# Three raw weight buffers, loads one piece further ahead, sums of w1 and w2 in common slabs, and first parts of w_out on ACT

## The chip, the core and the metric

The kernel runs on one core of one Trainium2 chip. The metric is device time in microseconds (us): the median over runs of the time from start to end of the program. Five engines share a core's on-chip memory: PE multiplies matrices, DVE and ACT work on tiles elementwise, POOL helps with copies, and SP issues the transfers from and to device memory.

## The reference: attention and two feed-forward layers

```python
# attention: q, k, v are (4, 8, 768, 64) float32; 4 sinks, a window of 128
scores = (1 / np.sqrt(64)) * np.matmul(q, k.transpose(0, 1, 3, 2))
keep = is_sink | in_window                      # column < 4, or 0 <= row - column < 128
scores = np.where(keep, scores, -1000000000.0)
a = np.exp(scores - np.max(scores, axis=-1, keepdims=True))
a = a / (np.sum(a, axis=-1, keepdims=True) + 1e-09)
x = np.matmul(a, v)                             # laid out as 3072 tokens x 512
h = np.maximum(x @ w_in, 0.0)                   # w_in 512 x 2048
x = (h * h @ w_out).astype(np.float32)          # w_out 2048 x 512
return ((x @ w1) * (x @ w2) @ w3) @ w_out2      # w1, w2 512 x 1024; w3 1024 x 1024; w_out2 1024 x 512
```

All weights arrive as float64, the rest as float32.

## The kernel before

**Stages.** The 3072 tokens are cut into 6 blocks of 512 (n = 0 to 5), and each block into 16 steps (j = 0 to 15), one per 128 columns of `w_in`. A step multiplies the block by its columns of `w_in` (`ffn_A`, 12 products into `hps`), applies the squared relu (`ffn_act1` to `ffn_act3`, which make `r` and `g`), and multiplies the step before by 128 rows of `w_out` (`ffn_B`, 12 products into `x1ps`). Between these stands one unit of attention, for the next block: score products into `sc`, masking and row maxima on DVE (`pr`), exponentials on ACT, a transpose by transfer (`pt<-ph`), the product with v into `y`, the division on DVE (`xn`), and a transposition on PE (`y<-ident,xn`). The unit runs as a pipeline over several steps, and the products with v and the transposition share the bank `y`. So a step's `y<-vp,pt` on PE can't start before DVE has read the bank's former content in `xn`; behind `y` on PE stands the next step's `hps`.

The prelude (0 to 94.6 us) computes the first 16 units in another way, directly in float32, and converts 12 weight pieces. Block n = 0 (94.6 to 212 us, called stage 0 here) converts the rest of `w_in` and `w_out`, 20 pieces, while it computes. Blocks 1 to 4 (212 to 610 us) convert two pieces of `w1` and `w2` each, in steps 4 and 5. Block 5 has no attention; it converts `w_out2` and the rest of `w1`, `w2`, and after it `w3` and `w_out2` are folded into one matrix (610 to 748 us). The rest (748 to 1108 us) is the second layer, in a form with seven block products in place of eight, for which sums of blocks of `w1` and `w2` are wanted.

**A weight piece.** A piece is 512 KB of float64. `f32_piece` (L1012) takes a buffer of the ring `raw64`, which has two, and has SP load it (L1029). `f64_to_f32_up` (L83) turns it into float32 in four instructions: ACT makes the magnitude (L86, `cvy<-raw`), DVE two integer pieces (L91 and L94, `cvt<-raw`) and merges them (L97, `cvy<-cvy,cvt`). The raw buffer is free once L86, L91 and L94 have read it. `split` (L795) then makes two half-precision parts: the first is a rounded copy of the float32 piece, by ACT or, where `hi_eng` is DVE, by DVE (CAST `wo<-cvy`); the second is the difference, on DVE or POOL (`wo<-cvy,wo`). `conv_wo` gives the first part of `w_out` to DVE in j = 0 to 7 and to ACT in j = 8 to 15.

**Ahead.** `w_load(upto)` issues loads up to a count, `w_conv` converts the next loaded piece. In the prelude and in blocks 0 to 4 the load of piece i + 2 is issued after the conversion of piece i. Block 5 does the same with a list of items (`item_load`).

**Sums.** `conv_w12` (L1221) waits for both pieces of a pair, then writes four sums of blocks (`s1` to `s4`) into one slab `w12s` of 128 x 1024, and splits that slab with one ACT and one DVE instruction. The ring `t2` has eight buffers of 128 x 512 float32, taken by `cvy`, `cvt`, the relu output `r` and others.

**What sets the order.** A scheduler orders the program by its own estimates. ACT, DVE and PE are written through a wrapper that keeps program order in blocks 0 to 4 (`InOrder`, L270), but the four instructions of `f64_to_f32_up` are not: they, SP and POOL are placed by the scheduler.

Of the kernel before, what the change touches and what calls it, by code (L numbers as in the profile page):

```python
# [7 lines left out]
F32 = mybir.dt.float32  # L8
F16 = mybir.dt.float16
BF16 = mybir.dt.bfloat16  # L10
I32 = mybir.dt.int32
# [285 lines left out]
def kernel(  # L297
# [18 lines left out]
    ACT, DVE, PE = (InOrder(tc, e, pinned) for e in (nc.scalar, nc.vector, nc.tensor))  # L316
# [4 lines left out]
    KD, KF, K2 = DM // 128, DFF // 128, DF2 // 128  # L321
# [18 lines left out]
    T2B, GB = 8, 3  # L340
# [25 lines left out]
    with ExitStack() as fast:  # L366
# [6 lines left out]
        def slab(tag, shape, dt, name, bufs=1):  # L373
            return big.tile(shape, dt, tag=tag, name=name, bufs=bufs)
# [420 lines left out]
        def split(src, hi, lo, lo_eng=None, hi_eng=None):  # L795

            if hi_eng is DVE:
                DVE.tensor_copy(out=hi, in_=src)
            else:
                ACT.activation(out=hi, in_=src, func=ACTF.Copy)  # L800
            (lo_eng or DVE).tensor_tensor(out=lo, in0=src, in1=hi, op=ALU.subtract)
# [9 lines left out]
        def ok(u):  # L811
            return 0 <= u < NU
# [204 lines left out]
        def f32_piece(src, dst=None, name="cv"):  # L1017

            if src.dtype == F32:
                if dst is None:  # L1020
                    dst = slab("t2", [128, 512], F32, name, bufs=T2B)
                SP.dma_start(out=dst, in_=src)
                return dst
            raw = slab("raw64", [128, 512, 2], I32, "raw64", bufs=2)
            fl = raw.rearrange("p n c -> p (n c)")
            sb32 = src.bitcast(I32)
            if len(sb32.shape) == 3:
                fl = fl.rearrange("p (a c) -> p a c", a=sb32.shape[1])
            SP.dma_start(out=fl, in_=sb32)  # L1029
            return raw  # L1030

        def conv(raw, dst=None):
            if raw.dtype == F32:
                ACT.activation(out=raw, in_=raw, func=ACTF.Copy, scale=W_UP)
                return raw
            y = slab("t2", [128, 512], I32, "cvy", bufs=T2B)
            if dst is None:
                dst = y.bitcast(F32)
            t = slab("t2", [128, 512], I32, "cvt", bufs=T2B)
            i = cvn[0]  # L1040
            cvn[0] += 1
            f64_to_f32_up(nc, raw, y, dst.bitcast(I32), st_w[:, i:i + 1], t)
            return dst
# [20 lines left out]
        def conv_wo(j):  # L1064
            c = j // 4
            if c not in wo_t:
                wo_t[c] = slab(f"wo{c}", [128, 2, 4, DM], F16, "wo")
            x = conv(raw_w.pop(("wo", j)))
            w = wo_t[c]
            split(x, w[:, 0, j % 4, :], w[:, 1, j % 4, :], hi_eng=DVE if j < KF // 2 else ACT)  # L1070

        hps_t = {}

# [150 lines left out]
        def conv_w12(i):  # L1224


            w12_x.append(conv(raw_w.pop(("w12", i))).rearrange("p (c f) -> p c f", c=KD))
            f, m = divmod(i, 2)
            if not m:
                return  # L1230
            x1, x2 = w12_x
            w12_x.clear()
            if f < 4:
                t = slab(f"w12_{f}", [128, 2, 7, 2, 128], F16, "w12")
                hi, lo = t[:, 0], t[:, 1]
            else:
                hi, lo = (slab(f"wi{2 * f - 8 + c}", [128, 7, 2, 128], F16, f"w12{c}") for c in range(2))
            w12_t[f] = hi, lo
            t = slab("w12s", [128, 4, 2, 128], F32, "w12s")
            s1, s2, s3, s4 = (t[:, c] for c in range(4))  # L1240
            a11, a12, a21, a22 = x1[:, 0:2], x1[:, 2:4], x2[:, 0:2], x2[:, 2:4]
            for o, p, q, op in (
                (s1, a21, a22, ALU.add), (s2, s1, a11, ALU.subtract), (s3, a11, a21, ALU.subtract),
                (s4, a12, s2, ALU.subtract),
            ):
                DVE.tensor_tensor(out=o, in0=p, in1=q, op=op)
            split(x1, hi[:, 0:2].rearrange("p a c f -> p (a c) f"), lo[:, 0:2].rearrange("p a c f -> p (a c) f"))
            split(a22, hi[:, 2], lo[:, 2])
            split(t, hi[:, 3:7], lo[:, 3:7])

        def x1_ops(o, top, bot):

# [125 lines left out]
        nl, ncv = [0], [0]  # L1378

        def w_load(upto):  # L1380
            while nl[0] < min(upto, len(pieces)):
                ld, _, j = pieces[nl[0]]
                ld(j)
                nl[0] += 1
# [36 lines left out]
        for h in range(2):  # L1421
# [1 line left out]
                out=vsf[h * NSINK:(h + 1) * NSINK, :, h, :],  # L1423
                in_=v[0].rearrange("(a h2) s d -> h2 s a d", h2=2)[h, 0:NSINK],
            )
        w_load(2)
        att_load_first(0, (0, 1, 2))
        if TBF > 2:
            att_load_first(1, (0, 1, 2))
# [3 lines left out]
        for u in range(UB + LEAD):  # L1433
            if 0 <= u - 3 < UB:
                att_norm(u - 3)
                att_X(u - 3)
                att_xT(u - 3)
            att_early(u)
            if u % 2 == 0 and u + 2 < UB:
                dir_T(u // 2 + 1)  # L1440
            if u < UB:
                dir_S(u)
                att_soft(u)
                att_exp(u)
            elif ok(u):
                att_S(u)
                att_soft(u)
                att_exp(u)
            if 0 <= u - 1 < UB:
                dir_P(u - 1)  # L1450
            if 0 <= u - 2 < UB:
                dir_O(u - 2)
            if ok(u - 2) and u - 2 >= UB:
                att_O(u - 2)
            if ok(u - 3) and u - 3 >= UB:
                att_X(u - 3)
            if ok(u) and u >= UB:
                att_P(u)
            for _ in range(2):
                if ncv[0] < L0 + 1:  # L1460
                    w_conv()
                    w_load(ncv[0] + 2)
            if u % TBF == 1 and u < UB:
                split_k(u // TBF)
            if u > TBF and (u - 1) % TBF == 0 and (u - 1) // TBF <= HP:
                split_v(u - 2)
# [4 lines left out]
        items = [(load_wo2, conv_wo2, i) for i in range(K2)]  # L1471
# [4 lines left out]
        def item_load(i):  # L1476
            items[i][0](items[i][2])
# [3 lines left out]
        for s in range(NK * KF):  # L1481
            n, j = divmod(s, KF)
            last = n == NK - 1
            e0, e1 = U0[n + 1] + LEAD, (U0[n + 2] if not last else U0[n + 1]) + LEAD
            us = list(range(uo, e0 + (e1 - e0) * (j + 1) // KF))
            uo = e0 + (e1 - e0) * (j + 1) // KF
            assert len(us) == (0 if last else 1)
            pinned[0] = not last
            if last and j == 0:
                low_att = att_verdict()  # L1490
                att_stack.close()
                late_p.append(fast.enter_context(tc.tile_pool(name="late", bufs=1)))
            ffn_A(n, j)
            for u in us:
                att_early(u)

            if n == 0:
                want = min(2 * KF, want0[j] + 1)
            elif not last:
                want = 2 * KF + 2 * (n - 1) + (j >= 4) + (j >= 5)  # L1500
            if last:
                if j == 0:
                    item_load(0)
                    item_load(1)
                items[j][1](items[j][2])
                item_load(j + 2)
            while not last and ncv[0] < want and ncv[0] < len(pieces):
                w_load(ncv[0] + 1)
                w_conv()
                w_load(ncv[0] + 2)  # L1510
            ffn_act1(n, j)
            for u in us:
                if ok(u):
                    att_S(u)
                    att_soft(u)
            ffn_sq(n, j)
            ffn_act2(n, j)
            for u in us:
                if ok(u):
                    att_exp(u)  # L1520
            ffn_act3(n, j)
            for u in us:
                if ok(u):
                    att_P(u)
            if pend:
                b = pend.pop()
                ffn_B(*b)
                if b[1] == KF - 1:
                    x1_spill(b[0])
            pend.append((n, j))  # L1530
            for u in us:
                if ok(u - 2):
                    att_O(u - 2)
                if ok(u - 3):
                    att_X(u - 3)
            if last:
                if j == KF // 2:
                    load_w3(0)
                w = wi_t[j][:, 0] if j < KF // 2 else wo_t[(j - KF // 2) // 2][:, 0, j % 2 * 2:j % 2 * 2 + 2]
                upper(w.rearrange("p c f -> p (c f)"))  # L1540
# [15 lines left out]
        for o, n in enumerate(order):  # L1556
            todo = []
            for f in range(K2):
                c = ffn_C(n, f)
# [14 lines left out]
                if f == 1 and o + 1 < NB:  # L1574
                    x = x1s_t[o + 1]
# [42 lines left out]
```

## Times and profile of the kernel before

| | us |
|---|---|
| median of 3 runs | 1110.32 (1108.42 to 1110.94) |
| the profiled execution | 1110.19 |
| its span, first to last instruction | 1108.0 |
| PE busy in the span | 1045.3 (94%) |
| DVE busy | 750.3 (68%) |
| ACT busy | 709.4 (64%) |
| POOL busy | 45.0 (4%) |

The profiled execution's time is its span and 2.2 us around it. The mean granted TensorE clock was 0.973 of full speed. Times in the rows below are us from the span's start, durations of groups are given as busy time and mean ns of one, and what stands in brackets behind an instruction is the idle time of its engine just before it, with what ended that.

### The profile page before, as it was taken

To read this page: it belongs to the slowest core of one execution; us is meant where nothing else is said; L and a number is where in the kernel's file an instruction comes from. 1 tells how busy PE (TensorE), PEld (TensorE's weight loads), DVE (VectorE), ACT (ScalarE), POOL (GpSimd) and SP (SyncE) were. 2 spreads that over 40 slices of the span, in tenths; PEclk is the share of its full clock that TensorE was granted. 3 is DMA by queue.
4 is the path that set the end of the run, shared out by engine and by line. 5 is a ranking of instruction groups with operands and counts; after the bars stand their busy time and mean duration, and the time that the engine had idled before them with its cause. 6 is when DMAs were issued, how large, how long until landed. Compare 5 with 4: busy or idle time off the path is not lost. (4 is left out here: it accounts for less than half of the span.)

```text
span 1108.0 us, 20449 instructions
## 1 busy us (share of the span) xinstructions
PE 1045.3 (94%) x7146; PEld 636.4 (57%) x7146; DVE 750.3 (68%) x2292; ACT 709.4 (64%) x1836; POOL 45.0 (4%) x163
## 2 busy tenths in 40 slices
PE   6777897999999999999999998999999999999996
PEld 5665443555555555555554444457767776777774
DVE  8797888887788888877865667945363636453433
ACT  6975688887667666766754877854464546454532
POOL 2110111000000000000000000000000000000000
PEclk9867999999999999999999999999999999999998
DMA  8876787786567657556833324421020201010101
GB/s 189 157 157 140 179 204 184 150 183 122 104 144 145 117 107 173 118 114 144 147 68 99 115 96 140 164 75 40 2 77 1 77 1 39 1 39 1 38 1 41
DMA packets 265535, 113.46 MB, mean 102 GB/s; under 512 B 237648, under 2 KB 254032, under 8 KB 264784
## 3 DMA queue, kind: packets, MB, share of 16 engines
q1 hardware_dynamic: 265136, 111.55, 43.7%
q8 instruction: 58, 0.95, 0.4%
q14 instruction: 53, 0.43, 0.2%
q10 hardware_dynamic: 288, 0.52, 0.1%
HBM read 62.08 MB, written 11.53 MB: 66 GB/s over the span
## 5 line engine op out<-in xcount | busy, mean ns | idle before, releaser
L288 PE MATMUL hps<-xT,wi 128*128 128x512 f16 x1152 | 270.9, 386 | 0.0
L288 PE MATMUL x1ps<-g,wo 128*128 128x512 f16 x1152 | 265.6, 380 | 3.0 <-ACT g L288 2.0
L288 PE MATMUL cps<-x1T,w 128*128 128x256 f16 x2016 | 231.5, 273 | 7.2 <-DVE cq L288 4.6
L288 PEld LDWEIGHTS <-w 128*128 128x128 f16 x2016 | 196.9, 98 | 44.5 <-issue 9.1
L288 PEld LDWEIGHTS <-wi 128*128 128x128 f16 x1152 | 115.0, 100 | 123.2 <-issue 8.6
L288 PEld LDWEIGHTS <-wo 128*128 128x128 f16 x1152 | 109.8, 98 | 122.6 <-issue 5.7
L288 PE MATMUL ops<-w,h 128*128 128x512 f16 x576 | 133.5, 379 | 1.8 <-ACT h L288 1.8
L288 ACT ACTIVATE cp<-cps 128x256 f32<-128x256 f32 x96 | 36.1, 376 | 131.3 <-PE cps L288 131.3
L288 ACT ACTIVATE r<-hps 128x512 f32<-128x512 f32 x96 | 56.8, 592 | 94.7 <-PE hps L288 94.7
L288 ACT ACTIVATE pr<-pr,stt 128x264 f32<-128x264 f32 (+1 forms) x176 | 77.6, 483 | 32.9 <-DVE stt L288 31.5
L288 PEld LDWEIGHTS <-h 128*128 128x128 f16 x576 | 56.2, 98 | 58.1 <-ACT h L288 2.1
L288 DVE TENSOR_TENSOR ph<-pr,ph 128x512 f16<-128x512 f32 (+2 forms) x148 | 59.2, 436 | 35.2 <-ACT ph L288 33.2
L288 DVE SCALAR_TENSOR_TENSOR asb<-cq,cps 128x256 f32<-128x256 f32 x48 | 20.2, 420 | 87.6 <-PE cps L288 87.6
L288 DVE CUSTOM_DVE_ANT_0 pr<-sc,mask 128x264 f32<-128x264 f32 (+1 forms) x176 | 65.2, 400 | 16.1 <-PE sc L288 15.5
L288 PEld LDWEIGHTS <-pt 128*128 128x128 f16 x956 | 40.3, 98 | 34.5 <-issue 17.1
L288 ACT ACTIVATE ph<-pr 128x512 f16<-128x512 f32 (+2 forms) x148 | 55.9, 421 | 5.8 <-DMA pt<-ph 3.4
L288 ACT ACTIVATE g<-r 128x512 f16<-128x512 f32 x88 | 55.3, 629 | 2.4
L288 DVE TENSOR_TENSOR g<-r,g 128x512 f16<-128x512 f32 x56 | 38.6, 689 | 24.6 <-ACT g L288 24.4
L97 DVE SCALAR_TENSOR_TENSOR cvy<-cvy,cvt 128x512 int32<-128x512 int32 x72 | 49.1, 688 | 8.5 <-ACT cvy L86 8.3
L288 PE MATMUL y<-vp,pt 128*128 128x65 f16 (+1 forms) x888 | 40.6, 195 | 14.7 <-DVE xn L288 14.6
L288 DVE TENSOR_TENSOR h<-asb,h 128x512 f16<-128x512 f32 x48 | 33.2, 691 | 28.2 <-ACT h L288 28.2
L288 PEld LDWEIGHTS <-qT 128*128 128x128 f16 x592 | 41.4, 99 | 18.9 <-issue 0.7
(193 smaller groups left out, 1490.3 us busy)
## 6 DMA issues: line engine op xcount, KB each, us to landing
raw<-in_moe_w_out_dram SPq DMA_DIRECT2D x24, 512.0 KB
raw<-in_moe_w_dram SPq DMA_DIRECT2D x24, 512.0 KB
raw<-in_moe_w_in_dram SPq DMA_DIRECT2D x16, 512.0 KB
raw<-in_k_dram SPq DMA_DIRECT2D x84, 64.0 KB
raw<-in_q_dram SPq DMA_DIRECT2D x84, 64.0 KB
raw<-in_v_dram SPq DMA_DIRECT2D x84, 64.0 KB
x_dr<-x1e SPq DMA_DIRECT2D x20, 256.0 KB
x1s<-x_dr SPq DMA_DIRECT2D x5, 1024.0 KB
```

The source lines that it names most:

```text
L97: nc.vector.scalar_tensor_tensor(out=dst, in0=y, scalar=3, in1=t, op0=ALU.logical_shift_left, op1=ALU.bitwise_or)
L288: r = f(*args, **kw)
```

## The change

The ring of raw buffers has three in place of two, and all loads are issued one piece further ahead: three at the start, and piece i + 3 after the conversion of piece i. ACT makes the first part of all 16 `w_out` pieces. The four sums of a pair go into two slabs of the ring `t2`, 128 x 512 each, in place of one slab of their own, and are split by two ACT and two DVE instructions of half the width. In block 5 three items are loaded at the start.

```diff
-            raw = slab("raw64", [128, 512, 2], I32, "raw64", bufs=2)
+            raw = slab("raw64", [128, 512, 2], I32, "raw64", bufs=3)
...
-            split(x, w[:, 0, j % 4, :], w[:, 1, j % 4, :], hi_eng=DVE if j < KF // 2 else ACT)
+            split(x, w[:, 0, j % 4, :], w[:, 1, j % 4, :], hi_eng=ACT)
...
-            t = slab("w12s", [128, 4, 2, 128], F32, "w12s")
-            s1, s2, s3, s4 = (t[:, c] for c in range(4))
+            t = [slab("t2", [128, 2, 2, 128], F32, "w12s", bufs=T2B) for _ in range(2)]
+            s1, s2, s3, s4 = (t[c // 2][:, c % 2] for c in range(4))
...
-            split(t, hi[:, 3:7], lo[:, 3:7])
+            for c in range(2):
+                split(t[c], hi[:, 3 + 2 * c:5 + 2 * c], lo[:, 3 + 2 * c:5 + 2 * c])
...
-        w_load(2)
+        w_load(3)
         att_load_first(0, (0, 1, 2))
...
                     w_conv()
-                    w_load(ncv[0] + 2)
+                    w_load(ncv[0] + 3)
...
                     item_load(1)
+                    item_load(2)
                 items[j][1](items[j][2])
-                item_load(j + 2)
+                if j + 3 < len(items):
+                    item_load(j + 3)
             while not last and ncv[0] < want and ncv[0] < len(pieces):
                 w_load(ncv[0] + 1)
                 w_conv()
-                w_load(ncv[0] + 2)
+                w_load(ncv[0] + 3)
```

The change moves instructions. At the start of the prelude, in SP's queue, this is the difference (L518 are the attention's first large loads):

```order
 L1029 DMA raw_183<-in_moe_w_in_dram 128x4x256
 L1029 DMA raw_185<-in_moe_w_in_dram 128x4x256
-L518 DMA raw_187<-in_k_dram 128x6x64 x2
-L518 DMA raw_190<-in_q_dram 128x6x64 x2
+L1029 DMA raw_187<-in_moe_w_in_dram 128x4x256
+L518 DMA raw_189<-in_k_dram 128x6x64 x2
+L518 DMA raw_192<-in_q_dram 128x6x64 x2
```

A third weight piece stands ahead of the attention's first large loads.

In SP's queue at the head of stage 0 the kernel before has this (qT, pt and `raw<-in_k` belong to the attention):

```order
L594 DMA_TRANSPOSE qT<-pkq 128x4x128
L1029 DMA raw_1408<-in_moe_w_out_dram 128x1024
L1029 DMA raw_1515<-in_moe_w_out_dram 128x1024
L738 DMA_TRANSPOSE pt<-ph_101 128x9x128
L1029 DMA raw_1525<-in_moe_w_in_dram 128x4x256
L506 DMA raw<-in_k_dram 128x2x64 x2
```

At the same place the changed kernel has this:

```order
L1029 DMA raw_1410<-in_moe_w_out_dram 128x1024
L1029 DMA raw_1517<-in_moe_w_in_dram 128x4x256
L1029 DMA raw_1527<-in_moe_w_out_dram 128x1024
L738 DMA_TRANSPOSE pt<-ph_101 128x9x128
L506 DMA raw<-in_k_dram 128x2x64 x2
```

The three loads that stood here begin with the piece that stood second, so each place in the queue carries the next piece.

On DVE, in one step of the middle of stage 0, the kernel before has this between the transposed tile `xT` and the packing of keys `pkk` (`den` is the row sum, `xn` the division):

```order
L288 TENSOR_TENSOR xT_1281<-y,xT_1280 128x128
L288 TENSOR_SCALAR den_1903<-y 128x2
L288 RECIPROCAL den_1903<-den_1903 128x2
L288 TENSOR_TENSOR xn<-y,den_1903 128x128
L288 SCALAR_TENSOR_TENSOR pkk<-raw,pkk 128x4x64 x2
```

In the same step the changed kernel has this (`ISA pr` is the masking with the row maximum):

```order
L288 TENSOR_TENSOR xT_1283<-y,xT_1282 128x128
L288 TENSOR_SCALAR den_1905<-y 128x2
L91 TENSOR_SCALAR cvt<-raw_1826 128x512
L288 ISA pr,stt<-sc,mask 128x128
L288 ISA stt 128x1
L94 TENSOR_SCALAR cvt<-raw_1826 128x512
L288 ISA pr,stt<-sc,mask 128x128
L288 ISA stt 128x1
L288 RECIPROCAL den_1905<-den_1905 128x2
L97 SCALAR_TENSOR_TENSOR cvy<-cvy,cvt 128x512
L288 TENSOR_SCALAR stt<-stt 128x2
L288 TENSOR_TENSOR xn<-y,den_1905 128x128
```

A conversion and the masking of the next unit have moved ahead of the division `xn` in this step. The two kernels have the same order on PE from stage 0 to the last block.

## Rows read from the trace of the kernel before

**Rows 1.** Windows by stage: start:end, length; then engines' busy time and columns named.
```profile
core 0: us, PE busy (x) PEld busy (x) DVE busy (x) ACT busy (x) POOL busy (x), PEclk, DMA share, GB/s
0.00:94.60 94.60, 69.40 (x420) 59.26 (x421) 77.25 (x358) 70.64 (x253) 14.90 (x50) 0.81 0.79 166
94.60:212.00 117.40, 103.07 (x686) 52.51 (x685) 98.21 (x318) 91.58 (x267) 11.36 (x31) 0.94 0.79 176
138.50:166.20 27.70, 25.52 (x178) 13.23 (x177) 24.34 (x76) 22.25 (x68) 3.30 (x7) 1.00 0.90 204
212.00:610.00 398.00, 398.00 (x2842) 210.73 (x2840) 310.03 (x1063) 272.76 (x687) 18.72 (x84) 1.00 0.62 128
610.00:748.00 138.00, 130.65 (x633) 63.16 (x632) 98.36 (x195) 103.08 (x218) 0.00 (x0) 0.99 0.35 118
0.00:27.70 27.70, 18.55 (x108) 15.27 (x109) 22.61 (x129) 18.51 (x65) 6.74 (x31) 1.00 0.81 189
```

**Rows 2.** Waits in stage 0 (94.6 to 212): total us, times, longest.
```profile
PE y L288 <- DVE xn L288: 13.4, 5, 3.6
...
DVE cvt L91 <- DMA raw<-in_moe_w_out_dram: 9.8, 5, 2.9
...
ACT cvy L86 <- DMA raw<-in_moe_w_out_dram: 8.2, 5, 2.8
...
ACT wo L288 <- DVE cvy L97: 2.9, 3, 2.2
```

**Rows 3.** Timeline of PE, 132 to 450: start, us, instruction, [idle before].
```profile
132.17 0.34 PE L288 MATMUL y<-vp,pt 128*128 128x65 f16 x6 [2.79 <-DVE xn L288]
...
132.50 4.44 PE L288 MATMUL hps<-xT,wi 128*128 128x512 f16 x12
...
192.84 0.34 PE L288 MATMUL y<-vp,pt 128*128 128x65 f16 x6 [2.29 <-DVE xn L288]
...
211.88 2.75 PE L288 MATMUL hps<-xT,wi 128*128 128x512 f16 x12
...
413.32 1.03 PE L288 MATMUL hps<-xT,wi 128*128 128x512 f16 x4
...
449.67 1.03 PE L288 MATMUL hps<-xT,wi 128*128 128x512 f16 x4
```

**Rows 4.** Timeline of DVE around the last gap of rows 3.
```profile
184.59 0.47 DVE L91 TENSOR_SCALAR cvt<-raw 128x512 uint16<-128x512 uint16 x1 [2.94 <-DMA raw<-in_moe_w_out_dram]
...
191.85 0.67 DVE L97 SCALAR_TENSOR_TENSOR cvy<-cvy,cvt 128x512 int32<-128x512 int32 x1
192.51 0.28 DVE L288 TENSOR_TENSOR xn<-y,den 128x128 f32<-128x128 f32 x1
```

**Rows 5.** Timeline of SP's queue: weight loads issued before that wait.
```profile
170.25 0.54 SPq L1029 DMA_DIRECT2D raw<-in_moe_w_in_dram  x1
...
180.44 0.52 SPq L1029 DMA_DIRECT2D raw<-in_moe_w_out_dram  x1
```

**Rows 6.** First part of w_out by engine, stage 0: busy, mean ns, idle before.
```profile
L288 DVE CAST wo<-cvy 128x512 f16<-128x512 f32 x6 | 2.5, 420 | 0.0
```

**Rows 7.** The same on ACT, stage 0.
```profile
L288 ACT ACTIVATE wo<-cvy 128x512 f16<-128x512 f32 x8 | 5.0, 624 | 2.9 <-DVE cvy L97 2.9
```

**Rows 8.** Splits of sums, and of a 512-wide piece, DVE, whole span.
```profile
L288 DVE TENSOR_TENSOR w<-w12s,w 128x1024 f16<-128x1024 f32 x8 | 9.8, 1220 | 1.8 <-ACT w L288 1.7
...
L288 DVE TENSOR_TENSOR w<-cvy,w 128x512 f16<-128x512 f32 x8 | 5.5, 688 | 4.8 <-ACT w L288 4.4 <-PE hps L288 0.4
```

**Rows 9.** Split of sums on ACT, whole span.
```profile
L288 ACT ACTIVATE w<-w12s 128x1024 f16<-128x1024 f32 x8 | 8.4, 1054 | 7.8 <-DVE w12s L288 7.6
```

**Rows 10.** Waits in the prelude (0 to 94.6).
```profile
DVE cvt L91 <- DMA raw<-in_moe_w_in_dram: 4.7, 3, 2.1
```

**Rows 11.** Timeline of PE in the prelude.
```profile
44.70 0.37 PE L288 MATMUL y<-ident,two 128*16 128x128 f32 x1 [1.89 <-DVE den L288]
...
54.96 0.33 PE L288 MATMUL y<-ident,xn 128*128 128x128 f32 x1 [1.64 <-DVE xn L288]
```

## The prediction

> **What bounds the kernel now.** I read the windows by stage first. From 212 to 610 us PE is busy in all of its 398.00 us, so there an edit on ACT or DVE changes nothing unless it makes PE wait [rows 1]. Stage 0 (94.6 to 212) is another matter: PE is busy in 103.07 of 117.40 us, and the DMA share is 0.79 there [rows 1]. How long it would take undisturbed can be read from later steps: the first product of a step starts at 413.32 and, six steps on, at 449.67, which is 36.35 / 6 = 6.06 us a step and 96.9 for 16 steps [rows 3]. Stage 0 is thus 117.4 - 96.9 = 20.5 us longer than its products need.
>
> The waits of stage 0 say where these go. PE stands 13.4 us before `y`, in five waits on DVE's division `xn` [rows 2]. The other 7.1 us are mostly products at the lower clock behind such a gap: twelve products take 4.44 us after the gap of 2.79, and 2.75 where the clock is full [rows 3]; the granted clock of the stage is 0.94, later 1.00 [rows 1].
>
> Why is `xn` late? DVE's own waits name it: five times, 9.8 us together, it stands before `cvt<-raw` for a piece of `w_out` that hasn't landed; ACT waits 8.2 us for the same pieces [rows 2]. With its 98.2 us of work DVE so accounts for 108.0 of the 117.4 us [rows 1, 2]: it paces this stage. The last of these waits shows the chain. DVE waits 2.94 us and goes on at 184.59; what is queued behind is late, `xn` comes at 192.51 behind a merge, and PE's `y` at 192.84 has waited 2.29 [rows 3, 4]. The piece was issued at 180.44, only 4.2 us before its use, though the weight load before it was issued at 170.25 [rows 4, 5]. A load needs a free raw buffer, and there are two: it is not issued because a buffer is still to be read.
>
> **The change part by part.** *Third buffer, loads one piece further, stage 0.* The order of SP shows the same places in the queue carrying the next piece. A piece that went out at 180.44 goes out at the place of 170.25, some 14 us before its use instead of 4.2. The five waits then end: 9.8 us off DVE's chain, which I take off the stage one for one, since DVE paces it. Does the transfer system have room? In 117.4 us its engines are busy for 0.79 x 117.4 = 92.7 us [rows 1]; in 117.4 - 9.8 = 107.6 us that is a share of 0.86, below the 0.90 that a stretch of 27.7 us held at 204 GB/s [rows 1]. At 204 GB/s the stage's bytes take 176 x 117.4 / 204 = 101.3 us, so 107.6 is to be had. Bounds: 0, where the wait comes back in another place, and -20.5, where every gap and every slow product goes. I take -9.8, the row that names the waits.
>
> *First parts of `w_out` on ACT.* In stage 0 six casts leave DVE, 2.5 us of work [rows 6], and ACT gets six at 0.624, 3.7 us [rows 7]. Beside -2.5 on DVE stands a new wait: in ACT's order a cast waits for DVE's merge, for which the eight casts that ACT has now waited 2.9 us, 0.36 each, so 2.2 for six [rows 2, 7]; behind it on ACT stand the relu output, exponentials and copies that DVE and PE want. ACT's work becomes 95.3 us, 89% of 107.6, and DVE's 95.7. Ends: -2.5, and 3.7 + 2.2 = +5.9 if ACT became the chain. What leaves DVE's chain and what comes to it by ACT's waits are 2.5 and 2.2, so I take 0; what covers the 3.7 us on ACT is the 8.2 us that it now waits for raw pieces [rows 2]. The Trainium skill, "ScalarE: Activation LUTs", section "Rules for kernel authors", speaks against this edit: simple elementwise work belongs on VectorE, not ScalarE. The rows agree on the single instruction, 0.42 on DVE and 0.62 on ACT, so by that rule the move costs 6 x 0.20 = 1.2 us and the sum would be 1101.3; the measured waits say that DVE is the engine to relieve here.
>
> *Prelude.* DVE waits 4.7 us, three times, for pieces of `w_in` [rows 10], and PE has two waits of 1.89 and 1.64 us on DVE's `den` and `xn` in the same stretch, 3.5 us [rows 11]; these end if the pieces come sooner. Against it the third load now stands ahead of the attention's first large loads: 512 KB at the 189 GB/s of the first 27.7 us are 2.8 us [rows 1], while nothing else can start. Ends -3.5 and +2.8; both rows count alike, so I take their sum, -0.7. A sentence of the Trainium skill bears on the second end: by "DMA: Bandwidth & Descriptors", section "Queues, rings and completion order", each DMA engine takes the descriptors of one ring in order, and by that alone, with nothing gained, the sum would be 1103.6. The trace of before shows no load in that place.
>
> *Sums in common slabs.* One DVE instruction of 1.22 us becomes two of 0.688 (+0.16) [rows 8], one of ACT's of 1.054 becomes two of about 0.62 (+0.19) [rows 7, 9], so +0.35 a pair. Four pairs lie between 212 and 610 under a PE that never waits: 0. The two slabs take turns in the ring `t2`, so the relu output `r` that comes next waits until DVE has made the difference that reads its buffer: 0 to 0.69 us [rows 8] in each of four blocks, 2.8 together. Behind `r` stand the square and `g`, and PE's `x1ps` waits for those. I take 0, for the same cover. If that cover fails, it is these 2.8 and 1.4 for the halves. The other four pairs lie in the last block, where PE is busy in 130.65 of 138.00 us [rows 1]; 4 x 0.35 = 1.4 times the idle share of 5% is +0.1. A sooner load there can't give back more than the 7.4 us of idle time; no wait of rows names a load, so 0.
>
> **The sum.** -9.8 + 0 - 0.7 + 0 + 0.1 = -10.4. The profiled execution took 1110.19 (span 1108.0 and 2.2 around it), so 1099.8; the median of before is 0.13 higher than that execution, which gives 1099.9.
>
> **Rivals.** *The gaps stay, for another reason.* In the changed order more divisions stand behind conversions: in the step shown, two masks, L91, L94 and L97 have come between `den` and `xn`, and of 14 divisions of stage 0 some nine stand like that, before about four or five. Two gaps with such a pattern are 2.79 and 2.29 [rows 3], 2.54 in the mean. If today's 13.4 us go and five new patterns cost 2.54 each, 12.7 come back: stage 0 gains 0.7, and with the prelude the time is 1108.9. Against it: the gaps of today come after a wait on data, and without it DVE reaches the conversion earlier than PE needs `xn`.
>
> *Slower.* Weights go ahead of what attention needs. In stage 0 three loads stand before `pt<-ph`; each holds the transfer engines for 512 KB / 204 GB/s = 2.6 us. If attention's transposes land later by what the weights land sooner, stage 0 gains nothing, the prelude pays its +2.8 and the halves their 1.4 without cover: 1110.3 + 4.2 = 1114.5. It decides from the point at which a transpose lands after PE has finished the `x1ps` before it. For it: a share of 0.81 in the prelude's first 27.7 us and of 0.90 in part of stage 0 [rows 1]. Against it: no transfer of attention is among the large waits of stage 0 [rows 2].
>
> *Much faster.* Without long gaps the clock stays up, and the 7.1 us of slow products go with the 13.4 us: -20.5 - 0.6, 1089.2. For it: a stretch of stage 0, 138.5 to 166.2, already holds a clock of 1.00 with PE busy in 25.52 of 27.70 us. Against it: DVE's 95.7 us of work would have to fit in 96.9 with hardly a wait.
>
> **How the numbers follow.** Chances: the forecast 0.57 (its own range 1095 to 1105: the prelude's and the casts' nearer ends), gaps that stay 0.12, slower 0.13, much faster 0.18. The range reaches from 1088.5, a little under the much faster case, to 1110.5, above the case of gaps that stay; it leaves out the slower case and part of the tail below, somewhat under 2 in 10. About 0.2%, or 2.2 us, is what a measurement of this kernel can tell from no change, so "same" is 1108.1 to 1112.5: 0.12. Faster is 0.57 + 0.18 = 0.75, slower 0.13.
>
> **What would show it.** Right: the wait of `cvt` on `w_out` in stage 0 falls from 9.8 us to under 2, PE's wait before `y` from 13.4 to about 6, the stage from 117.4 to about 107.6, and 212 to 610 keeps its length. The casts' step is wrong if ACT's waits on `cvy` grow by more than 2.5 us or PE waits on ACT's `r` or `g`. The prelude's is wrong if the first `kqps` or `sc` waits grow by 3 us. The forecast as a whole is wrong if the raw waits go and PE's wait on `xn` stays, or if the share of the transfer engines is no higher and the pieces still arrive late.

## The result, and the profile after

The changed kernel takes 1096.62 us (median of 4 runs, 1092.68 to 1099.57) against 1110.63 before: a ratio of 0.9868, with a 95% interval of 0.9825 to 0.9911. (The ratios are taken over the runs and aren't exactly those of the medians, here 0.9874.) Timed a second time on another occasion it stood at 0.9869 (0.9848 to 0.9890). Its profiled execution has a span of 1093.6 us, 14.4 less than before.

First the windows by stage of the changed kernel, cut at the first product `hps` of block 0 and of block 1, with columns as in [rows 1]. Block 1 now begins at 197.24 instead of 211.88.

```profile
0.00:93.73 93.73, 67.28 (x419) 58.39 (x420) 76.38 (x356) 71.82 (x255) 19.18 (x50) 0.85 0.79 173
93.73:197.24 103.51, 97.41 (x685) 50.52 (x684) 93.42 (x312) 93.87 (x272) 14.35 (x31) 0.99 0.91 197
197.24:595.36 398.12, 398.12 (x2843) 211.01 (x2841) 310.32 (x1067) 273.55 (x692) 19.06 (x84) 1.00 0.61 128
595.36:733.40 138.04, 130.32 (x633) 63.26 (x632) 97.98 (x199) 102.48 (x221) 0.00 (x0) 0.99 0.34 113
```

These rows show where the 14.4 us are: blocks 1 to 4, still without any gap of PE, and the last block with the fold have kept their lengths to 0.3 us (block 1 to the end is 1108.0 - 211.88 = 896.1 before and 1093.6 - 197.24 = 896.4 now). Stage 0 is shorter by 13.8 us and the prelude by 0.8. The transfer engines' share of stage 0 rose from 0.79 to 0.91, and the granted clock of PE there from 0.94 to 0.99.

The waits of stage 0 in the changed kernel, which answer to [rows 2]:

```profile
PE y L288 <- DVE xn L288: 4.7, 6, 2.2
...
ACT wo L288 <- DVE cvy L97: 2.7, 5, 0.8
DVE wo L288 <- ACT wo L288: 2.1, 4, 0.8
...
PE y L288 <- DMA pt<-ph: 0.9, 1, 0.9
...
DVE cvt L91 <- DMA raw<-in_moe_w_out_dram: 0.4, 1, 0.4
```

DVE's wait on raw weights has gone from 9.8 us to 0.4, PE's before `y` on DVE from 13.4 to 4.7. ACT's wait for raw pieces is gone. What came in its place is small: 0.9 us before `y` on attention's transpose. On the timeline of PE only one long gap is left, and the products behind it take 2.75 us, where twelve of them took 4.44 in [rows 3]:

```profile
106.08 0.52 PE L288 MATMUL y<-vp,pt 128*128 128x65 f16 x12 [2.17 <-DVE xn L288]
...
106.61 2.75 PE L288 MATMUL hps<-xT,wi 128*128 128x512 f16 x12
```

### The profile page after: what moved, and what is told of

Same layout as the page of the kernel before. It is cut to its first block, busy times and chain, and to the rows that moved or that the text cites. A ratio compares the mean times of both kernels' runs of the same rounds, so it can differ in the third digit from the quotient of the medians.

```text
span 1093.6 us, 20448 instructions
## 1 busy us (share of the span) xinstructions
PE 1037.3 (95%) x7146; PEld 634.2 (58%) x7146; DVE 744.9 (68%) x2292; ACT 713.4 (65%) x1852; POOL 52.6 (5%) x163
## 5 line engine op out<-in xcount | busy, mean ns | idle before, releaser
L288 PE MATMUL hps<-xT,wi 128*128 128x512 f16 x1152 | 265.2, 380 | 0.0
L288 PEld LDWEIGHTS <-w 128*128 128x128 f16 x2016 | 197.1, 98 | 44.3 <-issue 9.0
L288 DVE TENSOR_TENSOR cr<-cq,cps 128x256 f32<-128x256 f32 x48 | 20.2, 420 | 47.0 <-ACT cq L288 47.0
```

The source lines that it names most:

```text
L288: r = f(*args, **kw)
```

## The experiments

All are compared with the kernel before on the same chip. The columns behind the ratio are read from one profile each, in us: "block 1 at" is the start of its first `hps`, "DVE raw" and "PE" are the waits in stage 0 of DVE on raw weights and of PE on anything, and "clock" is the granted clock of stage 0.

| kernel | ratio to before (95%) | prelude | stage 0 | block 1 at | DVE raw | PE | clock |
|---|---|---|---|---|---|---|---|
| before | 1 | 94.6 | 117.3 | 211.9 | 9.8 | 14.3 | 0.94 |
| changed | 0.9868 (0.9825 to 0.9911) | 93.7 | 103.5 | 197.2 | 0.4 | 5.8 | 0.99 |
| changed, again | 0.9869 (0.9848 to 0.9890) | 91.9 | 105.2 | 197.0 | 0 | 5.3 | 0.97 |
| loads and slabs | 0.9898 (0.9875 to 0.9920) | 95.8 | 105.3 | 201.0 | 0 | 5.3 | 0.96 |
| the same, again | 0.9886 (0.9863 to 0.9908) | 94.1 | 103.8 | 197.9 | 0 | 4.9 | 0.97 |
| casts alone | 0.9986 (0.9971 to 1.0002) | 92.9 | 114.2 | 207.1 | 8.2 | 14.1 | 0.96 |
| slabs alone | 1.0004 (0.9988 to 1.0020) | 95.3 | 114.8 | 210.2 | 7.9 | 13.0 | 0.94 |
| all but the lead | 0.9919 (0.9900 to 0.9937) | 90.5 | 107.9 | 198.4 | 3.1 | 9.0 | 0.98 |
| lead from stage 0 on | 0.9875 (0.9843 to 0.9906) | 93.0 | 104.1 | 197.1 | 0 | 7.0 | 0.99 |
| all casts on DVE | 0.9901 (0.9871 to 0.9931) | 93.6 | 106.0 | 199.6 | 0.8 | 9.3 | 0.99 |
| conversions in order | 1.0225 (1.0194 to 1.0257) | 86.5 | 143.2 | 229.7 | 0 | 31.8 | 0.87 |
| four buffers | 0.9903 (0.9874 to 0.9932) | 94.6 | 106.2 | 200.8 | 0 | 6.6 | 0.97 |
| differences on POOL | 0.9915 (0.9885 to 0.9944) | 92.6 | 104.3 | 196.9 | 0 | 7.3 | 0.99 |
| third buffer alone | 0.9856 (0.9839 to 0.9873) | 90.6 | 103.4 | 194.0 | 0 | 7.3 | 1.00 |

**How far one profile can be read.** The changed kernel, unaltered.

> The changed kernel unaltered, timed again beside the run with loads alone on one chip, with a second profile. It shows how far one profile's stage lengths can be read: if stage 0 comes within 1 us of 103.5 and the prelude within 1 us of 93.7, differences of 2 us between kernels' profiles mean something; if not, they don't. Time 1096 to 1097.

Its stage 0 came at 105.2 and its prelude at 91.9, 1.7 and 1.9 us off; the two together agree to 0.2. With loads and slabs, whose two profiles are 3.2 us apart at block 1, it is no better. Behind block 1 too the second profile is longer, 898.5 us against 896.4. So a difference of 2 to 3 us between two profiles proves nothing by itself; the ratios have to carry it.

For the 1.7 us of stage 0 a place can be named. The long gap of PE is the same, 2.18 us here and 2.17 above, but the products behind it ran at a granted clock of 0.50 here and of 1.00 there:

```profile
105.21 0.52 PE L288 MATMUL y<-vp,pt 128*128 128x65 f16 x12 [2.18 <-DVE xn L288]
...
105.73 4.44 PE L288 MATMUL hps<-xT,wi 128*128 128x512 f16 x12
```

**Loads and slabs without the casts**, twice.

```diff
-            split(x, w[:, 0, j % 4, :], w[:, 1, j % 4, :], hi_eng=ACT)
+            split(x, w[:, 0, j % 4, :], w[:, 1, j % 4, :], hi_eng=DVE if j < KF // 2 else ACT)
```

> Three raw buffers, loads one piece further ahead and the common slabs, while DVE keeps the first parts of w_out in steps 0 to 7. Theory A (the loads are the whole gain): stage 0 about 104 us as in the changed kernel (before 117.3), time about 1097. Theory B (the casts carry part of it): stage 0 about 106 to 108, time 1099 to 1101, DVE busy there 2.5 us more.

> The loads and slabs without the casts' move, again, beside the changed kernel on the same chip. Theory A (DVE paces stage 0, so the six casts count by their 2.5 us): stage 0 at 105 to 106, and a ratio to the kernel before that is 0.002 to 0.004 above that of the changed kernel. Theory B (ACT's new waits take back what the casts free): the two ratios agree within 0.001.

Without the casts' move the raw waits are gone just so. The ratio is 0.0017 to 0.0030 above that of the changed kernel, with intervals that overlap: some 2 us for the casts are likely by this pair alone and not shown.

**Casts alone, slabs alone**, in the kernel before.

> The kernel before with only the first parts of w_out all on ACT; two raw buffers. Theory A: stage 0 stays at 116 to 118 us, since DVE still waits some 10 us for raw pieces, time 1110. Theory B: stage 0 falls by 2.5 us or more, time 1107 or less.

> The kernel before with only the sums of w1 and w2 in the common ring. Theory A: nothing before 600 us changes, 212 to 610 keeps its 398.1 us, the last block and the fold stay within 0.5 us, time 1110. Rival: the wait of the relu output on the ring shows in blocks 1 to 4, up to +2.8 us.

The casts alone leave 8.2 us of raw waits and are worth 0 to 3 us by their interval; the slabs alone are worth nothing. Stage 0 took 114.2 and 114.8 us in these profiles. The slabs are used only after it, so 117.3, from the single profile of the kernel before, may be some 2 us on the long side. No wait of the ring reached PE: in the profile with the slabs alone it is busy in all of the 399.85 us from 210.15 to 610.

**All but the lead.** The changed kernel with its loads two pieces ahead.

```diff
-        w_load(3)
+        w_load(2)
...
-                w_load(ncv[0] + 3)
+                w_load(ncv[0] + 2)
```

> The changed kernel, but loads are issued two pieces ahead, as before; only the third buffer stays. Theory A1 (what mattered was the buffer that is still to be read): loads go out without a wait for a buffer, stage 0 about 106, time about 1099. Theory A2 (what mattered is the earlier place in the queue): stage 0 stays above 113, raw waits of DVE above 6 us, time above 1106.

The third buffer without the lead, beside the casts and slabs, brings most of the gain, as theory A1 said. One raw wait is left. DVE's timeline of this kernel has it, and SP's queue shows why:

```profile
108.37 0.46 DVE L94 TENSOR_SCALAR cvt<-raw 128x512 uint16<-128x512 uint16 x1
...
123.30 0.46 DVE L91 TENSOR_SCALAR cvt<-raw 128x512 uint16<-128x512 uint16 x1 [3.13 <-DMA raw<-in_moe_w_out_dram]
```

```profile
99.55 0.34 SPq L1029 DMA_DIRECT2D raw<-in_moe_w_out_dram  x1
...
115.09 1.04 SPq L506 DMA_DIRECT2D raw<-in_k_dram  x2
116.19 1.74 SPq L506 DMA_DIRECT2D raw<-in_q_dram  x2
117.97 0.98 SPq L506 DMA_DIRECT2D raw<-in_v_dram  x2
118.99 0.47 SPq L1029 DMA_DIRECT2D raw<-in_moe_w_out_dram  x1
```

DVE had read a buffer out at 108.8, but the next load stands behind transposes and the six loads of attention that are shown, goes out at 118.99 and is wanted 4.3 us later, at 123.30. Here it is the place in SP's queue that is late, not the buffer. Against the second timing of the changed kernel the intervals are apart: beside casts and slabs the lead is worth some 5 to 6 us.

**Lead from stage 0 on.** Two loads at the start of the prelude, as before, three pieces ahead only in the blocks.

> The changed kernel, but in the prelude two loads at the start and two pieces ahead, as before; three pieces ahead only from stage 0 on. Theory A (the third load at the start delays attention's first transfers, which costs the prelude some 2 to 3 us): the prelude ends at about 90.5 us as in the run with the third buffer alone (changed kernel 93.7), stage 0 stays at 103 to 105, time 1093 to 1095. Rival (the prelude's length is set by how the scheduler lays its order, not by that load): the prelude ends anywhere between 90 and 96, and the first waits of PE on attention's keys stay at about 5 us.

The prelude ended at 93.0, between the two profiles of the changed kernel, and the ratio, 0.9875, lies within its interval. The third load at the start costs nothing that can be seen, so theory A fails. The prelude's end lies in the rival's range; but it moved by 1.9 us between two profiles of one program too, so that the laid order sets it is not shown.

**All casts on DVE**, the doubled dose.

> The changed kernel with the first parts of all 16 pieces of w_out on DVE. It doubles the dose against the run with loads alone. Theory A (the casts' place is worth 2 us or less of stage 0 for eight of them): stage 0 about 107, DVE busy 5 to 6 us more there than in the changed kernel, time 1098 to 1100. Theory B (casts cost nothing where the data is there): stage 0 stays at 103 to 105, time 1096.

DVE worked 6.2 us more in stage 0 than in the changed kernel, and the stage was 0.8 to 2.5 us longer. The ratio, 0.9901, has an interval that holds those with six casts on DVE and begins just above that with none, whose own interval overlaps it. So the fourteen casts may cost some 3.6 us, less than their busy time; that they cost anything is not shown.

**Conversions in program order.**

```diff
-            f64_to_f32_up(nc, raw, y, dst.bitcast(I32), st_w[:, i:i + 1], t)
+            f64_to_f32_up(pin_nc, raw, y, dst.bitcast(I32), st_w[:, i:i + 1], t)
...
```

(`pin_nc` has the wrappers of ACT and DVE for engines.)

> The changed kernel with the four instructions of each conversion kept in program order too in blocks 0 to 4, so that none stands between the divisor and the division by the scheduler's choice. Theory A (what is left of PE's wait before y, 4.7 us, is conversions ahead of the division): PE's wait before y in stage 0 falls to 2 us or less, stage 0 to 100 to 102, time 1093 to 1095. Rival (the scheduler's places are the better ones, since program order puts conversions in a lump): stage 0 goes up by 2 us or more.

The rival was right, by far more than it said: stage 0 takes 143.2 us. These are its waits there:

```profile
PE hps L288 <- ACT r L288: 31.8, 8, 6.3
ACT wo L288 <- DVE cvy L288: 21.2, 15, 2.4
...
ACT wi L288 <- DVE cvy L288: 17.9, 8, 2.4
DVE wo L288 <- ACT wo L288: 10.4, 15, 0.7
```

ACT and DVE wait for one another within each piece, the relu output `r`, which frees the bank `hps`, stands behind that on ACT, and PE waits for the bank. Only 9 pieces instead of 12 are converted before stage 0, which accounts for a part of its length. But blocks 1 to 4, with the same pieces as ever, take longer too: block 5 begins 394.3 us after block 1, and 388.6 in the changed kernel. So the conversions gain from being strewn between other work. PE's wait on `xn` has gone, but with PE late in another place that says little of its cause; what the conversions cost in a lump is far more.

**Four buffers**, loads one piece further ahead again.

```diff
-            raw = slab("raw64", [128, 512, 2], I32, "raw64", bufs=3)
+            raw = slab("raw64", [128, 512, 2], I32, "raw64", bufs=4)
...
```

> The changed kernel with four raw buffers and loads one piece further ahead again, from the start and in blocks 0 to 4. Theory A (three buffers end the waits, and the transfer engines are busy 0.91 of stage 0): stage 0 stays within 2 us of 103.5, the prelude gets longer by up to 2.8 us by a fourth load at the start, time 1096 to 1099. Rival (each further piece ahead helps): stage 0 falls below 101, time below 1094.

Stage 0 took 106.2 us, 1.1 and 2.7 above the two profiles with three buffers, and the ratio is not better: theory A, if anything with a small loss. There was no raw wait left to take. Of the 7.2 us by which the span of this profile exceeds that of the changed kernel, only half lies before block 1; where the rest comes from is open.

**Differences on POOL.** Every other second part of `w_out` is made by POOL.

```diff
-            split(x, w[:, 0, j % 4, :], w[:, 1, j % 4, :], hi_eng=ACT)
+            split(x, w[:, 0, j % 4, :], w[:, 1, j % 4, :], POOL if j % 2 else DVE, ACT)
```

> The changed kernel with the second parts of every other piece of w_out made by POOL instead of DVE: seven or so instructions of 0.69 us leave DVE in stage 0, 4.8 us, and as many of 1.16 us go to POOL. Theory A (DVE paces stage 0: its busy time, its waits on raw data and some 10 us more are its length): DVE busy about 89, stage 0 at 99 to 101, time 1092 to 1094. Rival (PE and ACT bind as well now, or POOL's work slows DVE's beside it): stage 0 stays at 102 to 105, time 1096.

Seven instructions left DVE, yet its busy time in stage 0 is 91.84, only 1.6 us less, and the stage takes 104.27:

```profile
92.63:196.90 104.27, 96.91 (x686) 50.72 (x685) 91.84 (x305) 93.91 (x272) 21.62 (x38) 0.99 0.88 195
```

So POOL's work slowed DVE's (last section). Theory A was not tested as it should be, since DVE was not relieved by 4.8 us; what is shown is that this way brings nothing. By the times it rather loses: this profile is of the fastest of six runs, whose median is 1099.13, while the changed kernel had 1096.02 on the same occasion; the two intervals barely overlap.

**The third buffer alone.** The kernel before with one number changed.

```diff
-            raw = slab("raw64", [128, 512, 2], I32, "raw64", bufs=2)
+            raw = slab("raw64", [128, 512, 2], I32, "raw64", bufs=3)
```

> The kernel before with one number changed: three raw buffers in place of two. Loads stay two pieces ahead in the code, casts and slabs as before. Theory A (a load waited for a buffer still to be read, and that is the whole cause): DVE's waits on raw data in stage 0 fall from 9.8 us to under 4, the first step of block 1 comes at 198 to 201 us instead of 211.9, time 1098 to 1100. Rival (it needs the load one piece further ahead, or the casts' move, as well): block 1 begins after 205 us, time 1104 or more.

It takes 1093.81 us against 1110.54, 0.9856 (0.9839 to 0.9873): as fast as the changed kernel or faster, and the lowest ratio of all. That is better than theory A said, which had block 1 at 198 to 201 and a time of 1098 to 1100; the profile is of the fastest of its five runs. Its prelude and stage 0, from its windows, and the waits that PE still has in stage 0:

```profile
0.00:90.63 90.63, 63.35 (x420) 52.82 (x420) 77.43 (x356) 70.05 (x252) 17.87 (x48) 0.89 0.80 178
90.63:193.99 103.36, 95.96 (x686) 50.40 (x684) 96.66 (x321) 91.27 (x268) 13.18 (x31) 1.00 0.91 200
```

```profile
PE y L288 <- DVE xn L288: 5.2, 5, 2.6
...
PE y L288 <- DMA pt<-ph: 1.1, 1, 1.1
PE y L288 <- DMA raw<-in_v_dram: 1.0, 1, 1.0
```

DVE does 3.2 us more work in stage 0 than in the changed kernel, since it has the casts, and yet the stage is not longer. No raw wait is among its waits. In SP's queue the load that went out at 118.99 in the kernel without the lead goes out at 113.18, ahead of attention's loads:

```profile
111.87 1.21 SPq L594 DMA_TRANSPOSE qT<-pkq  x1
113.18 0.52 SPq L1029 DMA_DIRECT2D raw<-in_moe_w_out_dram  x1
113.80 1.19 SPq L738 DMA_TRANSPOSE pt<-ph  x1
115.08 1.05 SPq L506 DMA_DIRECT2D raw<-in_k_dram  x2
```

The code says "two pieces ahead" in both; the scheduler lays the queue otherwise when casts and slabs differ. With these two edits left out the kernel is faster by 0.6% (0.9856 against 0.9919, intervals apart). Of the 6.0 us between the two spans 4.4 lie before block 1, where the one raw wait of 3.1 us is; which of the two edits moves the load was not tested.

## Why the prediction was right, and where it was off

It forecast 1099.9 in a range of 1088.5 to 1110.5, and 1096.6 came; -10.4 us was forecast and -14.0 came by the medians.

**The chain of stage 0: right.** Raw pieces came late for want of a buffer; DVE stood, `xn` came late, PE stood before `y`. The third buffer alone ends it, which is the direct test: the raw waits fall from 9.8 us to 0, PE's wait on `xn` from 13.4 to 5.2, and stage 0 gets 14.0 us shorter (the prelude 3.9).

**What held the loads: read too simply.** Of the load at 180.44 the prediction says that it is not issued because a buffer is still to be read. It takes the buffer whose last reads in the kernel before are these, on ACT and DVE:

```profile
175.15 0.67 ACT L86 ACTIVATE cvy<-raw 128x512 f32<-128x512 f32 x1
```

```profile
175.63 0.45 DVE L94 TENSOR_SCALAR cvt<-raw 128x512 uint16<-128x512 uint16 x1
```

From 176.08 on the buffer was free, and SP's queue issued attention's transposes:

```profile
175.04 1.30 SPq L738 DMA_TRANSPOSE pt<-ph  x1
176.51 2.52 SPq L555 DMA_TRANSPOSE kT<-pkk  x2
179.13 1.21 SPq L594 DMA_TRANSPOSE qT<-pkq  x1
180.44 0.52 SPq L1029 DMA_DIRECT2D raw<-in_moe_w_out_dram  x1
```

The other four loads that DVE waited for, issued at 103.20, 119.05, 124.22 and 152.21, also went out 2.6 to 5.3 us after the last read of their buffers. So when they went out it was their place in SP's queue that held them, as in the kernel without the lead. Loads between them did wait for a buffer, and what stood behind in the queue waited too: SP issued nothing from 165.13 to 167.31, where the next load's buffer had its last read at 167.19. The number of buffers bears on both, for the scheduler laid SP's queue otherwise when that one number changed; how much each counts for was not separated.

**Its size: too small, -9.8 against -13.8 and -12.2 in two profiles.** That more came than -10.4 in all doesn't hang on the profiles: the second timing's interval, 0.9848 to 0.9890, is a gain of 12.2 to 16.9 us. The mis-sized step is "9.8 us off DVE's chain, which I take off the stage one for one". Of the 20.5 us of excess in stage 0, the forecast let the slow products stay. PE's waits fall from 14.3 us to 5.8, which is 8.5; and what is left over the 96.9 us of undisturbed steps and the waits falls from 6.1 us to 0.8 (2.9 in the second profile, nothing for the third buffer alone, at a clock of 1.00), which is the other 5.3. The "much faster" case said so, but wanted all gaps gone; the truth lies between the two. That the transfer engines have room was right: a share of 0.91 was held through the stage, hardly above the 0.90 that was read from a part of it before.

The slow products behind a gap are thus part of its price, though not each time: the two profiles of the changed kernel differ there behind the same gap. Nor are all slow products behind gaps of stage 0. Before, its first 4 us already ran at a clock of 0.50, as the prelude had ended; by an estimate that is 2 us of the 6.1 (4.00 us of products at half speed):

```profile
94.56:98.56 4.00, 4.00 (x11) 1.47 (x10) 2.52 (x9) 1.10 (x3) 0.18 (x2) 0.50 0.54 106
```

**The casts at 0: supported, not settled.** As in [rows 7] a cast on ACT takes 0.62 us; the fourteen of stage 0 wait 2.7 us for DVE's merge, 0.19 each, where 0.36 was read, and DVE in turn waits 2.1 us for ACT. Alone they are worth 0 to 3 us, with the lead some 2 to 3 by ratios whose intervals overlap, and without it nothing favourable: the kernel that leaves them, and the slabs and the lead, out has the lowest ratio. The prediction's other sum for this edit, 1101.3, is 0.2 too high: 1099.9 and 1.2 are 1101.1.

**The prelude at -0.7: -0.8 and -2.7 measured.** DVE's wait there for `w_in` fell from the 4.7 us of [rows 10] to 1.7. The feared cost of the third load at the start didn't appear: PE's first waits before `kqps` were 4.5 us in the kernel before and are 5.2 and 4.6 in the two profiles. The lengths of these preludes differ by more than the forecast's whole term, so its parts are not shown, and that the first came so close is luck. The Trainium skill, "DMA: Bandwidth & Descriptors", section "Queues, rings and completion order", states that each DMA engine takes the descriptors of a ring in order; that the load so delays what stands behind it, no run here shows. The prediction's sum for that case, 1103.6, is 0.2 too high as well: 1099.9, 0.7 and 2.8 are 1103.4.

**The slabs at 0: right.** Blocks 1 to 4 keep 398.1 us, the ring's wait doesn't reach PE, and the halves cost as worked out (DVE 0.686, ACT 0.620 each) where nothing waits for them.

**The rivals.** Gaps that stay by conversions ahead of the division: five of the six waits on `xn` that remain have a conversion between `den` and `xn`, but they take 2.5 us together, 0.5 each, where 2.54 each was feared; the sixth, of 2.17, has `xn` close behind its `den`. Weights ahead of attention's transfers: 0.9 us before `y` on a transpose, nothing like 4.2.

**What stays open.** Whether the lead and the casts cost or gain anything beside a third buffer: their effects, some 2 to 7 us by the ratios, differ in sign with what they are combined with, and each edit also brings a new order of SP's queue.

## What to carry to other kernels

Where an engine waits for a load that was issued only a few microseconds before its use, look for what held the issue: a buffer still to be read, or its place in the queue. Three times tell them apart: the last read of the buffer, the issue, and what the queue issued between them. Change the number of buffers by itself first; here one number gave the whole gain, and three further edits with it gave no more. And count what a gap does to the work behind it: where products run at a lower clock after it, they belong to its price.

## What the runs showed of the hardware that was not expected

Where a subtraction of POOL on a tile of 128 x 512 runs beside an operation of DVE on two such tiles, one of the two is stretched. The rival of that run had named it; its size was not known. In the kernel with differences on POOL, here first POOL's and then DVE's timeline:

```profile
160.52 1.16 POOL L801 TENSOR_TENSOR wo<-cvy,wo 128x512 f16<-128x512 f32 x1
```

```profile
160.72 1.50 DVE L288 TENSOR_TENSOR ph<-pr,ph 128x512 f16<-128x512 f32 x1 [1.36 <-ACT ph L288]
```

DVE's instruction takes 1.50 us where its like take 0.69. Where DVE's began first, at 132.23 in the same trace, it kept its 0.68, and POOL's, from 132.41 on, took 1.52 instead of 1.16. By the groups of DVE in stage 0 the seven differences that left took 6.0 us with them (10.8 to 4.8), but `ph` rose from 8.2 us to 10.9 and `g` from 11.0 to 11.8. The Trainium skill, "Perfetto Trace Analysis", section "Optimizing Scalar/DVE Operations", says that the two engines share a read port of the on-chip memory, so that moving work between them might not help. The trace agrees that it didn't, with these numbers; that the port is the cause no run here shows.
